# The last 64 rows of w_down as 128 half rows on all partitions, and no closing barrier

## The chip, the cores and the metric

The kernel runs on one core of a Trainium2 chip. The metric is the device time of one execution in microseconds (us). "Span" is the time from the first to the last recorded instruction of the core; the device time is longer than the span (1288.06 against 1286.26 us in the profiled run of the kernel before), and this text calls that difference the gap. A partition is one row of the on-chip memory: the first index of a tile in the code, 0 to 127. In the profile's lines PE is TensorE (PEld its weight loads), DVE is VectorE, ACT is ScalarE, POOL is GpSimd and SP is SyncE; a q behind the name means the engine's sequencer, which also issues the loads (SPq DMA_DIRECT2D in the profile, 328 to 548 ns each for the four loads of the feed-forward weights).

## The reference, cut to what matters

```python
xn = layernorm(x)                                    # x: [1, 1, 640]
att = softmax(q @ k.T / sqrt(128)) @ v               # 32 heads, 32768 cached keys and values of 128, bf16
y  = x + att.reshape(1, 1, 4096) @ wo \
       + (silu(xn @ w_gate) * (xn @ w_up)) @ w_down  # w_gate, w_up: [640, 1728]; w_down: [1728, 640]
```

One token is decoded. 554 MB of keys, values and weights are read once. 1728 hidden units are 13 full blocks of 128 and a rest of 64 (FM = 13, FB = 14, FL = 64 in the code).

## The kernel before

One DMA queue, issued by SyncE, streams everything in a fixed order into a ring of three slots. The end of the order is: last values, w_gate, w_up, w_down, then wo in six pieces. The loads of the feed-forward weights:

```python
e.dma_start(wg, B_w_gate.rearrange("(p c) n -> p (c n)", c=NCD)).then_inc(s_ffn[0], 16)
e.dma_start(wu, B_w_up.rearrange("(p c) n -> p (c n)", c=NCD)).then_inc(s_ffn[1], 16)
e.dma_start(flat[:, d0:d0 + FM * D], B_w_down[0:FM * 128, :].rearrange(
    "(p j) n -> p (j n)", j=FM)).then_inc(s_ffn[2], 16)
e.dma_start(wd[0:FL, FM, :], B_w_down[FM * 128:F, :]).then_inc(s_ffn[2], 16)   # 64 rows of 1280 B
# ... then six pieces of wo, of 8, 8, 8, 5, 2 and 1 rows of 640 per partition
e.wait_ge(s_fin, 2)
e.dma_start(out[0, 0:1, :].rearrange("o (c m) -> (o c) m", c=NCD), orow[:, :]).then_inc(s_out, 16)
```

TensorE multiplies with the weights as the stationary operand, so that all results are columns; the last block has only 64 rows:

```python
def down():
    t.wait_ge(s_ffn[2], 32)
    t.wait_ge(s_fd, 8)
    # ...
    for j in range(FB):
        n = 128 if j < FM else FL
        for c in range(NCD):
            t.matmul(acc[:, c:c + 1], lhsT=wd_v[0:n, j, c, :], rhs=hcol[0:n, j:j + 1], ...)
```

GpSimd builds constants at the start and at the end waits for the output write (`g.wait_ge(s_out, 16)`). After the engines' own streams the language puts a closing barrier: each engine drains and raises a semaphore, GpSimd collects the four and releases all. (In the records four engines have a drain, of 152 to 322 ns, and a semaphore record from 1273.2 to 1285.3 us; GpSimd's two follow at 1286.1 and 1286.2, the second one of the four at 1286.2.)

## Time and profile before

| what | value |
|---|---|
| time, median of 3 runs | 1288.11 us (1288.03 to 1288.64) |
| span, profiled run | 1286.3 us |
| bytes read | 554 MB at 431 GB/s over the span |
| last piece of wo in the queue | issued at 1254.4, landed 28.9 us later, about 1283.3 |
| output write issued | 1284.63 |
| GpSimd's branch to the closing barrier | 1285.9 |
| last record | 1286.26 |

Lines of the profile's page: the span; the mean busy share of the 16 DMA engines in 40 equal slices, in tenths; bytes.

```profile
span 1286.3 us, 9864 instructions
...
DMA  9999999999999999999999999999999999999998
...
HBM read 553.99 MB, written 0.00 MB: 431 GB/s over the span
```

The DMA row stays at 9, so there is no compute to be saved. Time can be won only where the queue moves fewer bytes than it could, or after its last byte.

The chain of waits at the end of the kernel before (start us, duration us, what):

```profile
1253.07 29.08 DMA ring<-in_A_wo_dram
1282.15 0.05 issue
1282.19 1.49 PE ps L414 x40
...
1283.81 0.17 DVE outb L603
...
1284.02 0.28 PE ps L439
...
1284.33 0.28 DVE orow L605
```

The chain is one long wait for wo. TensorE's last 40 matmuls stretch over 1.49 us because they contain the waits for the last two pieces: they start 27 ns apart, but 0.13 us where those land, at 1282.94 and 1283.33. Then comes a fixed tail.

Busy time by stretches of 1 us, kernel before. Columns: stretch; length; busy us and number of instructions of PE, PEld, DVE, ACT, POOL; granted clock; mean busy share of the DMA engines; GB/s moved.

```profile
1266.00:1267.00 1.00, 0.62 (x10) 0.63 (x11) 0.00 (x0) 0.00 (x0) 0.00 (x0) 0.50 1.05 449
...
1268.00:1269.00 1.00, 1.00 (x18) 0.97 (x18) 0.00 (x0) 0.20 (x1) 0.00 (x0) 0.50 1.01 329
1269.00:1270.00 1.00, 1.00 (x20) 1.00 (x20) 0.00 (x0) 0.00 (x0) 0.00 (x0) 0.50 1.01 323
1270.00:1271.00 1.00, 1.00 (x20) 1.00 (x19) 0.00 (x0) 0.00 (x0) 0.00 (x0) 0.50 0.96 340
1271.00:1272.00 1.00, 1.00 (x20) 1.00 (x20) 0.00 (x0) 0.00 (x0) 0.00 (x0) 0.50 0.98 399
```

The last two columns are the finding: for 3 us the DMA engines are fully busy and move a fifth less. That is when the 64-row piece, 80 KB, passes.

The records of the closing barrier, all on the line of the enclosing block (engine's sequencer, operation, count; ns min/median/max; start of the first and the last in us):

```profile
L79 SPq EVENT_SEMAPHORE  x2: 17/17/17, 1285.3 to 1286.2; - x2
L79 POOLq EVENT_SEMAPHORE  x2: 17/17/17, 1286.1 to 1286.2; - x2
...
L79 POOLq COMPARE_BRANCH  x1: 33/33/33, 1285.9 to 1285.9; - x1
```

SyncE is done at 1285.3 and is released at 1286.2. GpSimd (POOL) comes last, at 1285.9, since it waited for the output write, whose last semaphore update is at 1285.82.

### The profile page before, as it was taken

The numbers are of one execution on the slowest core, as the hardware profiler recorded it, in microseconds if no ns is written. First come the engines' busy times: TensorE is split into PE (matmuls) and PEld (weight loads), VectorE is DVE, ScalarE is ACT, GpSimd is POOL, SyncE is SP. The second block draws the span as 40 slices with busy tenths as digits, with TensorE's granted clock in tenths as the row PEclk, the third lists the DMA queues.
The fourth block names the chain that finished last, engine by engine and source line by source line (L and its number), as shares of the span: only waits on it lengthen the run. The fifth ranks groups of instructions, "written<-read, shape, count | busy, mean of one in ns | idle before, by whom it ended". The sixth has DMA issues, their size and how long they took to land.

```text
span 1286.3 us, 9864 instructions
## 1 busy us (share of the span) xinstructions
PE 1041.6 (81%) x5153; PEld 261.4 (20%) x3234; DVE 670.4 (52%) x409; ACT 52.2 (4%) x140; POOL 2.5 (0%) x17
## 2 busy tenths in 40 slices
PE   4599777789777788777798777788777798778797
PEld 1011112221112221112221112221112221112227
DVE  0855665445665445664446664446664446654440
ACT  2000000000000000000000000000000000000000
POOL 0000000000000000000000000000000000000000
PEclk9799888898888999888898888898888998888895
DMA  9999999999999999999999999999999999999998
GB/s 424 424 450 427 429 438 431 430 430 444 428 432 442 428 432 434 436 428 432 442 430 432 436 432 430 430 444 428 432 442 428 432 432 438 428 432 442 430 417 355
DMA packets 11192, 554.17 MB, mean 431 GB/s; under 512 B 1259, under 2 KB 1452, under 8 KB 1708
## 3 DMA queue, kind: packets, MB, share of 16 engines
q1 hardware_dynamic: 11178, 554.00, 99.7%
q8 instruction: 9, 0.15, 0.0%
q14 instruction: 3, 0.02, 0.0%
q10 hardware_dynamic: 2, 0.00, 0.0%
HBM read 553.99 MB, written 0.00 MB: 431 GB/s over the span
## 4 chain that ended last, share of the span: by engine, by line
DMA 53%; PE 30%; DVE 11%; issue 6%; DVEq 0%; SPq 0%
DMA ring<-in_A_k_cache_dram 51%; PE ps L327 17%; PE ps L295 11%; DVE ring L543 10%; DMA ring<-in_A_wo_dram 2%; PE ps L314 1%; PE ps L369 0%; PE ps L363 0%; PE ps L357 0%; PE ps L414 0%; SPq L239 0%; DVEq L543 0%; DVE sc L549 0%; DVE pmax L555 0%; DVEq L188 0%
## 5 line engine op out<-in xcount | busy, mean ns | idle before, releaser
L543 DVE TENSOR_TENSOR ring<-ring,qb 128x8192 bf16<-128x8192 bf16 x128 | 557.8, 4420 | 316.4 <-DMA ring<-in_A_k_cache_dram 316.4
L295 PE MATMUL ps<-ring,ident 128*128 128x512 bf16 x1920 | 496.4, 417 | 0.0
L327 PE MATMUL ps<-ring,P 128*4 128x512 bf16 x1984 | 443.3, 379 | 0.0
L314 PE MATMUL ps<-ring,ident 128*128 128x512 bf16 x128 | 55.9, 437 | 220.7 <-DVE ring L543 220.2
L327 PEld LDWEIGHTS ps<-ring,P 128*4 128x4 bf16 x1984 | 163.4, 85 | 237.8
L314 PEld LDWEIGHTS ps<-ring,ident 128*128 128x128 bf16 x128 | 12.6, 98 | 618.0 <-DVE ring L543 345.0
L549 DVE TENSOR_REDUCE sc<-ps 128x64 f32<-128x512 f32 x128 | 82.3, 684 | 62.6 <-PE ps L295 62.6
L561 DVE TENSOR_SCALAR negb<-ps 128x1 f32<-128x1 f32 x32 | 5.1, 158 | 108.4 <-PE ps L369 108.4
L466 ACT ACTIVATE P<-sc,negb 128x256 bf16<-128x256 f32 x32 | 16.2, 507 | 956.7 <-DVE negb L561 956.7
L558 DVE TENSOR_REDUCE m<-ps 1x1 f32<-1x128 f32 x32 | 8.9, 278 | 85.2 <-PE ps L363 85.2
L349 PEld LDWEIGHTS ps<-identf,o 4*128 4x128 f32 x248 | 30.6, 190 | 13.1 <-issue 13.1
L349 PE MATMUL ps<-identf,o 4*128 4x1 f32 x248 | 33.2, 251 | 0.0
L357 PEld LDWEIGHTS ps<-rsum,ones 128*128 128x128 f32 x64 | 12.1, 190 | 99.0 <-issue 98.2
L457 ACT ACTIVATE o<-ps,rzb 4x512 f32<-4x512 f32 x31 | 21.0, 678 | 6.2 <-PE ps L327 6.2
L287 PE MATMUL ps<-ring 128*128 128x512 bf16 x39 | 11.3, 458 | 10.9 <-DMA ring<-in_A_wq_dram 10.9
L462 ACT ACTIVATE ocol<-ps 128x1 f32 (+1 forms) x31 | 5.4, 173 | 222.2 <-PE ps L349 222.2
L555 DVE TENSOR_REDUCE pmax<-sc 128x1 f32<-128x256 f32 x32 | 13.4, 420 | 0.0
L363 PE MATMUL ps<-identf,pmax 128*1 128x128 f32 x64 | 12.2, 273 | 1.2 <-DVE pmax L555 1.2
L369 PE MATMUL ps<-m,ones 1*128 1x1 f32 x64 | 12.1, 256 | 0.4 <-DVE m L558 0.4
L369 PEld LDWEIGHTS ps<-m,ones 1*128 1x128 f32 x64 | 9.4, 182 | 14.2 <-issue 13.5
L393 PE MATMUL ps<-xn,ring 128*128 128x1 bf16 (+1 forms) x140 | 8.9, 198 | 1.6 <-issue 1.6
L531 DVE RECIPROCAL rzb<-ps 128x1 f32<-128x1 f32 x32 | 5.1, 159 | 8.1 <-PE ps L357 8.1
(62 smaller groups left out, 80.8 us busy)
## 6 DMA issues: line engine op xcount, KB each, us to landing
ring<-in_A_wq_dram SPq DMA_DIRECT2D x1, 5120.0 KB, 15.3
ring<-in_A_v_cache_dram SPq DMA_DIRECT2D x1, 4096.0 KB, 31.8
ring<-in_A_wo_dram SPq DMA_DIRECT2D x3, 1280.0 KB, 25.0
ring<-in_B_w_gate_dram SPq DMA_DIRECT2D x1, 2160.0 KB, 22.9
ring<-in_B_w_up_dram SPq DMA_DIRECT2D x1, 2160.0 KB, 27.7
ring<-in_B_w_down_dram SPq DMA_DIRECT2D x1, 2080.0 KB, 31.7
ring<-in_A_v_cache_dram SPq DMA_DIRECT2D x1, 2048.0 KB, 36.4
ring<-in_A_v_cache_dram SPq DMA_DIRECT2D x2, 1024.0 KB, 39.4
```

The source lines that it names most:

```text
L295: return t.add_instruction(mybir.InstMatmult(start_tensor_calc=False, stop_tensor_calc=stop, tile_size=(128, 128), tile_position=(0, 0), l ...
L314: t.matmul(ob, lhsT=ident[:, :], rhs=src, start=True, stop=False)
L327: mm = t.matmul(O, lhsT=P[:, h % PR, j:j + W], rhs=ring[:, s, j * DH:(j + W) * DH], start=(j == 0), stop=(j + W == NJ))
L349: mm = t.matmul(fold_ps, lhsT=o4[:, m * DH:(m + 1) * DH], rhs=identf[0:W, m:m + 1], start=(m == 0), stop=(m == W - 1))
L357: t.matmul(misc[:, 129:130], lhsT=ones[:, :], rhs=rsum[:, h % SR:h % SR + 1], start=True, stop=True).then_inc(s_z, 1)
L363: t.matmul(misc[0:1, 0:128], lhsT=pmax[:, h % SR:h % SR + 1], rhs=identf[:, :], start=True, stop=True).then_inc(s_t, 1)
L369: t.matmul(misc[:, 128:129], lhsT=ones[0:1, :], rhs=m1[0:1, h % SR:h % SR + 1], start=True, stop=True).then_inc(s_b, 1)
L457: a.activation(out=o4[:, :], in_=O, func=ACTF.Copy, scale=rzb[0:W, h % SR:h % SR + 1]).then_inc(s_o4, 1)
L466: a.activation(out=P[:, h % PR, :], in_=sc[:, :], func=ACTF.Exp, bias=negb[:, h % SR:h % SR + 1], scale=c_scale, accum_out=rsum[:, h % SR: ...
L543: v.tensor_tensor(out=kh, in0=kh, in1=q[:, None, :].to_broadcast([128, HF, DH]), op=ALU.mult).then_inc(s_mul, 1)
L549: v.tensor_reduce(out=sc[:, i * HF:(i + 1) * HF], in_=bank[i].rearrange("p (j e) -> p j e", e=G), axis=AX.X, op=ALU.add).then_inc(s_red, 1)
L555: v.tensor_reduce(out=pmax[:, h % SR:h % SR + 1], in_=sc[:, :], axis=AX.X, op=ALU.max).then_inc(s_max, 1)
```

## The change

Intent: let the last 64 rows of w_down use all 128 partitions, as the other loads of the feed-forward weights do, and let each engine end with its own stream. Row f becomes two half rows on partitions 2f and 2f + 1. Each hidden unit of the last block must then stand on two partitions, too. So VectorE doubles the last 64 columns of w_gate and w_up, and the last hidden column is masked by the parity of the partition into two columns, one for each half of the outputs. Core of the diff, with cuts:

```diff
-                        e.dma_start(wd[0:FL, FM, :], B_w_down[FM * 128:F, :]).then_inc(s_ffn[2], 16)
+                        e.dma_start(wdr, B_w_down[FM * 128:F, :].rearrange(
+                            "f (t n) -> (f t) n", t=2)).then_inc(s_ffn[2], 16)
 ...
+                    for half in range(2):
+                        a, b = half * (D // 2), (half + 1) * (D // 2)
+                        for c in range(a // 128, (b + 127) // 128):
+                            m0, m1 = max(a, c * 128), min(b, c * 128 + 128)
+                            t.matmul(acc[m0 - c * 128:m1 - c * 128, c:c + 1], lhsT=wdr[:, m0 - a:m1 - a],
+                                     rhs=hcol[:, FM + half:FM + half + 1],
+                                     start=False, stop=False, skip_group_check=True)
 ...
+                def twice(i):
+                    v.wait_ge(s_ffn[i], 16)
+                    v.tensor_copy(out=wt[i].rearrange("p c (f t) -> p c f t", t=2),
+                                  in_=(wg_v, wu_v)[i][:, :, FM * 128:F][:, :, :, None].to_broadcast(
+                                      [128, NCD, FL, 2])).then_inc(s_twice, 1)
 ...
+                v.tensor_reduce(out=par[:, :], in_=ident[:, :].rearrange("p (f t) -> p t f", t=2),
+                                axis=AX.X, op=ALU.add).then_inc(s_fd, 1)
 ...
+                v.tensor_scalar(out=hcol[:, FM:FM + 2], in0=par[:, :], scalar1=sg[:, 0, FM:FB],
+                                scalar2=ffn[:, FB + FM:2 * FB], op0=ALU.mult, op1=ALU.mult).then_inc(s_fd, 1)
 ...
+    nc.main_func.blocks[-1].instructions = []
```

The gate arithmetic also becomes one piece of 14 columns instead of two pieces (13 columns, and 64 rows of one).

More of the change, by code (lines that the diff above doesn't have):

```diff
@@ L98, in bass_parallel_sum__gqa_block_cached__swiglu_ffn__decode_kernel @@
         ot = sbt("ot", [128, OC], BF16)
-        hcol = sbt("hcol", [128, FB], BF16)
+        hcol = sbt("hcol", [128, FB + 1], BF16)
+        par = sbt("par", [128, 2], F32)
         sg = sbt("sg", [128, 2, FB], F32)
@@ L131, in bass_parallel_sum__gqa_block_cached__swiglu_ffn__decode_kernel @@
         s_att, s_fin = sem("att"), sem("fin")
+        s_twice = sem("twice")
         s_xr, s_or = sem("xr"), sem("orow")
@@ L160, in bass_parallel_sum__gqa_block_cached__swiglu_ffn__decode_kernel @@
         d0 = f0 + 2 * NCD * F
-        wd = flat[:, d0:d0 + FB * D].rearrange("p (j d) -> p j d", j=FB)
-        assert 2 * NCD * F + FB * D <= CE
+        wd = flat[:, d0:d0 + FM * D].rearrange("p (j d) -> p j d", j=FM)
+        wdr = flat[:, d0 + FM * D:d0 + FM * D + D // 2]
+        assert 2 * NCD * F + FM * D + D // 2 <= CE and 2 * FL == 128 and D % 2 == 0
         wg_v = wg.rearrange("p (c n) -> p c n", c=NCD)
@@ L165, in bass_parallel_sum__gqa_block_cached__swiglu_ffn__decode_kernel, with hidden @@
         wd_v = wd.rearrange("p j (c m) -> p j c m", c=NCD)
-        def hidden(w, c, j):
+        u0 = d0 + FM * D + D // 2
+        wt = [flat[:, u0 + i * NCD * 128:u0 + (i + 1) * NCD * 128].rearrange("p (c m) -> p c m", c=NCD)
+              for i in range(2)]
+        assert u0 + 2 * NCD * 128 <= f0 + CE
+        def hidden(i, c, j):
+            w = (wg_v, wu_v)[i]
             if j < FM:
                 return w[:, c, 0:FM * 128].rearrange("p (m j) -> p m j", j=FM)[:, :, j]
-            return w[:, c, FM * 128:F]
+            return wt[i][:, c, :]
         wo = flat[:, WO_S * CE:WO_S * CE + OC * D]
@@ L388, in hidden_part @@
                     t.wait_ge(s_ffn[i], 16)
-                    w = (wg_v, wu_v)[i]
                     for j in range(FB):
-                        n = 128 if j < FM else FL
+                        if j == FM:
+                            t.wait_ge(s_twice, i + 1)
                         for c in range(NCD):
-                            mm = t.matmul(ffn[0:n, i * FB + j:i * FB + j + 1], lhsT=hidden(w, c, j),
+                            mm = t.matmul(ffn[:, i * FB + j:i * FB + j + 1], lhsT=hidden(i, c, j),
                                           rhs=xn[:, c:c + 1], start=(c == 0), stop=(c == NCD - 1))
@@ L398, in down @@
                     t.wait_ge(s_ffn[2], 32)
-                    t.wait_ge(s_fd, 8)
-                    first = True
-                    for j in range(FB):
-                        n = 128 if j < FM else FL
+                    t.wait_ge(s_fd, 6)
+                    for j in range(FM):
                         for c in range(NCD):
-                            t.matmul(acc[:, c:c + 1], lhsT=wd_v[0:n, j, c, :], rhs=hcol[0:n, j:j + 1],
-                                     start=first, stop=False, skip_group_check=True)
-                            first = False
+                            t.matmul(acc[:, c:c + 1], lhsT=wd_v[:, j, c, :], rhs=hcol[:, j:j + 1],
+                                     start=(j == 0 and c == 0), stop=False, skip_group_check=True)
+                    for half in range(2):
[5 more added lines that the diff above has]
+                                     start=False, stop=False, skip_group_check=True)
                 def project():
@@ L489, in act @@
                 a.wait_ge(s_f, 1)
-                a.activation(out=sg[:, 0, 0:FB - 1], in_=ffn[:, 0:FB - 1], func=ACTF.Exp,
-                             scale=-1.0).then_inc(s_fa, 1)
-                a.activation(out=sg[0:FL, 0, FB - 1:FB], in_=ffn[0:FL, FB - 1:FB], func=ACTF.Exp,
-                             scale=-1.0).then_inc(s_fa, 1)
+                a.activation(out=sg[:, 0, :], in_=ffn[:, 0:FB], func=ACTF.Exp, scale=-1.0).then_inc(s_fa, 1)
             @block.vector
@@ L573, in dve @@
                 rz(H - 1)
+                def twice(i):
[3 more added lines that the diff above has]
+                                      [128, NCD, FL, 2])).then_inc(s_twice, 1)
+                twice(0)
                 h = H - 1
@@ L582, in dve @@
                                 in1=blk[:, None, :].to_broadcast([128, H, RB]), op=ALU.mult).then_inc(s_ob, 1)
-                v.wait_ge(s_fa, 2)
-                pieces = [(slice(0, 128), slice(0, FM)), (slice(0, FL), slice(FM, FB))]
-                n = 0
-                for stage in range(4):
-                    for p, f in pieces:
-                        fu = slice(FB + f.start, FB + f.stop)
-                        if stage == 0:
-                            ins = v.tensor_scalar(out=sg[p, 0, f], in0=sg[p, 0, f], scalar1=1.0, scalar2=None,
-                                                  op0=ALU.add)
-                        elif stage == 1:
-                            ins = v.reciprocal(out=sg[p, 1, f], in_=sg[p, 0, f])
-                        elif stage == 2:
-                            ins = v.tensor_tensor(out=sg[p, 0, f], in0=sg[p, 1, f], in1=ffn[p, f], op=ALU.mult)
-                        else:
-                            ins = v.tensor_tensor(out=hcol[p, f], in0=sg[p, 0, f], in1=ffn[p, fu], op=ALU.mult)
-                        ins.then_inc(s_fd, 1)
-                        n += 1
-                    v.wait_ge(s_fd, n)
+                twice(1)
+                v.tensor_reduce(out=par[:, :], in_=ident[:, :].rearrange("p (f t) -> p t f", t=2),
+                                axis=AX.X, op=ALU.add).then_inc(s_fd, 1)
+                v.wait_ge(s_fa, 1)
+                v.tensor_scalar(out=sg[:, 0, :], in0=sg[:, 0, :], scalar1=1.0, scalar2=None,
+                                op0=ALU.add).then_inc(s_fd, 1)
+                v.wait_ge(s_fd, 2)
+                v.reciprocal(out=sg[:, 1, :], in_=sg[:, 0, :]).then_inc(s_fd, 1)
+                v.wait_ge(s_fd, 3)
+                v.tensor_tensor(out=sg[:, 0, :], in0=sg[:, 1, :], in1=ffn[:, 0:FB], op=ALU.mult).then_inc(s_fd, 1)
+                v.wait_ge(s_fd, 4)
+                v.tensor_tensor(out=hcol[:, 0:FM], in0=sg[:, 0, 0:FM], in1=ffn[:, FB:FB + FM],
+                                op=ALU.mult).then_inc(s_fd, 1)
+                v.tensor_scalar(out=hcol[:, FM:FM + 2], in0=par[:, :], scalar1=sg[:, 0, FM:FB],
+                                scalar2=ffn[:, FB + FM:2 * FB], op0=ALU.mult, op1=ALU.mult).then_inc(s_fd, 1)
                 v.wait_ge(s_xr, 1)
```

## The prediction

> **What bounds it.** The kernel streams 554 MB at a mean of 431 GB/s over a 1286.3 us span, the page's DMA row at 9 tenths in nearly every slice: the DMA queue bounds it from start to end. The engines matter only after the last byte. In the chain of waits the end is: the projection weights (wo) land piece by piece (1282.15, then two smaller ones by about 1283.3), 40 last matmuls (1282.19 to 1283.68), one DVE add, one transposing matmul, one DVE cast, output DMA issued at 1284.63, GpSimd sees it landed at 1285.85, then the closing barrier: branch 1285.91, last semaphore records of all engines at 1286.2.
>
> **What the change removes.**
> 1. The 64-row piece of w_down (64 x 1280 B, partitions 0 to 63). It is only 80 KB, about 0.2 us at 430 GB/s, but the table by 1 us stretches shows 329, 323 and 340 GB/s in 1268 to 1271, with all engines busy, against 399 to 450 around it: about 250 KB missing, 0.6 us. Packet durations in the trace agree: in 1267 to 1272 packets take 0.73 us per DMA engine more than the shortest of their size, mostly the big neighbours (10240 B: 385 ns, up to 879 here), on all 16 engines. [...] As 128 half rows of 640 B [...] this goes away. Price: 128 small packets instead of 64; from 1280 B = 55 ns and 2560 B = 102 ns I estimate 32 ns for 640 B, so 0.25 instead of 0.22 us per engine. Net about -0.6 us, and it lies on the critical path: all of wo queues behind it.
> 2. The closing barrier: 1285.91 to 1286.26, about -0.3 us at the end of the span. What the runtime does outside the span (1288.06 less 1286.3 = 1.8 us) I expect about unchanged.
>
> **What it adds, off the critical path.** Two DVE copies of 128x640 bf16 (the like copy at the start took 0.82 us): one at about 1260 when w_gate has landed, before DVE is needed at 1262.5; one at about 1265.2 when w_up has landed, before PE needs it near 1268 to 1272. One 128x128 reduce in DVE's idle time. One more matmul in the down projection (71 for 70), two more waits on PE that are already met. The gate arithmetic loses four small DVE operations and one ACT operation. PE had 1.6 us of idle time (1278.6 to 1280.2) before it waited for wo; about 1 us of that remains.
>
> **Prediction.** 1288.1 - 0.6 - 0.35 - a little = 1287.0 us, range 1286.3 to 1287.7. Chance of faster by over 2%: 0.005; within 2%: 0.99; slower: 0.005.
>
> **What would show it.** Throughput in 1268 to 1271 at about 400 GB/s or more; wo landing 0.6 us earlier; PE still waiting for wo; the last record GpSimd's; span about 1285.3.
>
> **What would make it wrong.** The slow stretch may not come from the 64-row piece, or only engines with slack recover, so wo lands only 0.2 us earlier; an instruction fetch stall of PE (1.7 us idle at 1264.8) may move behind the down projection and eat the slack; the runtime's own end may wait as long as the barrier did, so its removal shows in the span but not in the time.

1288.1 less 0.6 (from the rates in 1268 to 1271), less 0.35 (the barrier), less a little comes to 1287.0 us. What the prediction calls an instruction fetch stall is an idle time of TensorE, from 1264.79 to 1266.38, that ended 1.4 us after an instruction packet of 16 KB (1263.90 to 1264.97); the profile names no releaser for it, so the link is the author's reading.

## The result, and the profile after

The changed kernel took 1287.47 us (median of 4 runs, 1287.11 to 1288.13), the kernel before 1288.07 us (1287.97 to 1288.64) in the same rounds: 0.6 us less, ratio 0.9995, interval 0.9978 to 1.0012. The span of the profiled run is 1285.6 us.

The same stretches in the kernel after:

```profile
1266.00:1267.00 1.00, 1.00 (x21) 1.00 (x19) 0.41 (x2) 0.00 (x0) 0.00 (x0) 0.50 1.09 466
...
1268.00:1269.00 1.00, 1.00 (x21) 1.00 (x19) 0.00 (x0) 0.00 (x0) 0.00 (x0) 0.50 1.02 416
1269.00:1270.00 1.00, 1.00 (x20) 1.00 (x19) 0.00 (x0) 0.00 (x0) 0.00 (x0) 0.50 0.98 391
1270.00:1271.00 1.00, 1.00 (x20) 1.00 (x19) 0.00 (x0) 0.00 (x0) 0.00 (x0) 0.50 1.05 431
```

The slow stretch is gone. The records of the single packets say the same: the loads' packets that start from 1267 to 1272 took 0.70 us per DMA engine (the sum over 16 engines, by 16) more than the shortest of their size before, and 0.06 us after. Linked end to start, the packets form 16 sequences; leaving out one packet beside an instruction fetch, each lost 0.62 to 0.77 us before, and at most 0.04 us after. What was added stays off the chain; VectorE's two copies, in the timeline after (start, duration, instruction, idle time before it and what ended that):

```profile
1260.26 0.82 DVE L588 COPY ring<-ring 128x640 bf16<-128x640 bf16 x1 [7.09 <-DMA ring<-in_B_w_gate_dram]
1265.40 0.82 DVE L588 COPY ring<-ring 128x640 bf16<-128x640 bf16 x1 [2.80 <-DMA ring<-in_B_w_up_dram]
```

They run in VectorE's idle time, each for the 0.82 us foreseen. The chain of waits after:

```profile
1253.03 28.77 DMA ring<-in_A_wo_dram
1281.80 0.05 issue
1281.85 1.49 PE ps L428 x40
```

It is the old chain with the wait for wo 0.35 us shorter (1282.15 to 1281.80). The prediction had 0.6. Part of the difference arises ahead of the changed piece. These are lines of the DMA view before (operation, KB, us from issue to landing; the issues' start times agree within 0.1 us):

```profile
ring<-in_B_w_gate_dram SPq DMA_DIRECT2D x1, 2160.0 KB, 22.9
...
ring<-in_A_wo_dram SPq DMA_DIRECT2D x1, 800.0 KB, 29.1
```

The same lines after:

```profile
ring<-in_B_w_gate_dram SPq DMA_DIRECT2D x1, 2160.0 KB, 23.2
...
ring<-in_A_wo_dram SPq DMA_DIRECT2D x1, 800.0 KB, 28.8
```

w_gate, which stands before the changed piece in the queue, landed 0.3 us later in this run. So the piece gave back about 0.6 us between w_gate's landing and wo's in this pair of profiles, and 0.3 of it had been lost before.

At the end the barrier's records are gone; this is all that is left on that line:

```profile
L79 POOLq COMPARE_BRANCH  x1: 33/33/33, 1285.5 to 1285.5; - x1
```

The span ends with GpSimd's branch: 0.7 us earlier in all, 0.38 of it the data and 0.32 the barrier (GpSimd's branch ended at 1285.944 before, the last record at 1286.259). But the time fell by only 0.6 us or less: the gap rose from 1.80 us (1288.06 less 1286.26) to 2.04 us (1287.60 less 1285.56). The experiments ask about both halves.

### The profile page after: what moved, and what is told of

Its sections match the earlier page's. It is cut to its first block, busy times and chain, and to the rows that moved or that the text cites. A ratio compares the mean times of both kernels' runs of the same rounds, so it can differ in the third digit from the quotient of the medians.

```text
span 1285.6 us, 9851 instructions
## 1 busy us (share of the span) xinstructions
PE 1042.0 (81%) x5154; PEld 260.9 (20%) x3235; DVE 672.2 (52%) x409; ACT 52.1 (4%) x139; POOL 2.5 (0%) x17
## 4 chain that ended last, share of the span: by engine, by line
DMA 53%; PE 28%; DVE 12%; issue 6%; SPq 0%; DVEq 0%
DMA ring<-in_A_k_cache_dram 51%; PE ps L337 17%; DVE ring L554 12%; PE ps L305 9%; DMA ring<-in_A_wo_dram 2%; PE ps L324 1%; PE ps L379 0%; PE ps L373 0%; PE ps L367 0%; PE ps L428 0%; SPq L249 0%; DVEq L554 0%; DVE sc L560 0%; DVE pmax L566 0%; DVE m L569 0%
## 5 line engine op out<-in xcount | busy, mean ns | idle before, releaser
L403 PE MATMUL ps<-xn,ring 128*128 128x1 bf16 x140 | 8.3, 196 | 1.3 <-issue 1.3
```

## The experiments

My theory of the load: the partitions that the 64 rows are written to, 0 to 63, slow them and their neighbours, not the size of the packets or the number of rows. Why they should was not shown: the reason that the recorded texts gave is cut from e4_rows_32_95 and x0_rows_0_63, and in the latter also a lower estimate for the ten copies that rested on it. In the trace of the kernel before, the piece's 64 packets form 16 runs of four, in which they start 47 to 84 ns apart, and each load of w_down raises its semaphore 16 times; I read that as four rows for each of the 16 DMA engines. Rivals: packet size or row count, the switch between transfers, or that all of the gain is the barrier. My theory of the end: the barrier's 0.32 us shows in the time; rival: the gap takes it back.

### Each half of the change alone, and both again

Edits, each against one of the two kernels:

```diff
 e1_no_barrier (the kernel before)
+    nc.main_func.blocks[-1].instructions = []
 e2_half_rows (the changed kernel)
-    nc.main_func.blocks[-1].instructions = []
 e3_both_again: the changed kernel, no edit
```

> Only the closing barrier is taken out; w_down's last 64 rows stay on partitions 0 to 63. My theory (the two parts add up, and the barrier's share shows in the measured time): span about 0.33 us shorter than before's 1286.3, time about 0.3 us shorter than the runs of before, 1267 to 1271 as slow as before (323 to 340 GB/s). Rival A (the runtime's own end waits as long): span 0.33 us shorter, time unchanged within 0.1 us. Rival B (the barrier is all of the gain): time 0.6 us shorter.

> Only the half rows, with the closing barrier kept. My theory: no slow stretch at 1267 to 1271; the last byte of wo lands 0.3 to 0.6 us earlier than in before, according to which DMA engines the instruction fetches of the tail hit; time 0.3 to 0.6 us shorter. Rival B (the barrier is all of the gain): time within 0.1 us of before.

> The changed kernel once more, as a control in the same rounds. My theory: time 0.6 to 0.9 us under before; if the shortfall against the predicted 1.05 us is only which DMA engine the instruction fetches hit, this profile's landing of w_gate (23.2 us after issue in the first profile of this kernel, 22.9 in before) may differ again, and the last wo landing moves with it. Sum rule: its gain equals that of e1_no_barrier plus that of e2_half_rows within 0.3 us.

### Whole rows on partitions 32 to 95

The load keeps its 64 packets of 1280 B. The compute takes 96 rows; 32 of the weight rows are zero. (A form with two matmuls of 32 rows each was not run.) Cut:

```diff
-                        e.dma_start(wd[0:FL, FM, :], B_w_down[FM * 128:F, :]).then_inc(s_ffn[2], 16)
+                        e.dma_start(wd[32:32 + FL, FM, :], B_w_down[FM * 128:F, :]).then_inc(s_ffn[2], 16)
-            return w[:, c, FM * 128:F]
+            return w[:, c, FM * 128 - 32:F]
 ...                                    # 64 becomes 96 rows in matmuls, exponential and gate arithmetic
+                v.memset(wd[0:32, FM, :], 0.0).then_inc(s_fd, 1)
+    nc.main_func.blocks[-1].instructions = []
```

> Whole rows again, 64 packets of 1280 B, but on partitions 32 to 95, computed with 96-row operands whose first 32 weight rows are zero, and no closing barrier. If the slow stretch comes from [...] (my theory), it is gone here too: packets of 10240 B at 385 to 395 ns, 400 GB/s or more at 1267 to 1271, and time as e3_both_again within 0.2 us or a little below. If it comes from the piece having 64 rows, or from its packet size, the stretch stays slow and the time is that of e1_no_barrier.

Measured in these rounds, five runs of each, before 1288.13 us (9 runs, 1287.92 to 1288.66):

| kernel | load of the 64 rows | barrier | time, median (range) | mean time less mean span |
|---|---|---|---|---|
| before | partitions 0 to 63 | yes | 1288.13 (1287.92 to 1288.66) | 1.81 |
| e1_no_barrier | partitions 0 to 63 | no | 1287.88 (1287.77 to 1288.29) | 1.98 |
| e2_half_rows | 128 half rows | yes | 1287.38 (1287.33 to 1287.42) | 1.80 |
| e3_both_again | 128 half rows | no | 1287.37 (1287.23 to 1287.47) | 2.00 |
| e4_rows_32_95 | partitions 32 to 95 | no | 1287.49 (1287.33 to 1287.72) | 2.03 |

With the barrier the half rows are worth 0.75 us, above the 0.3 to 0.6 expected for this run, and without it 0.51 us (e1_no_barrier against e3_both_again); the prediction had 0.6. That the barrier is all of the gain is refuted. Taking the barrier out as well adds 0.01 us, on the old load it adds 0.25: both little, neither the 0.35 predicted. The two gains add up within the 0.3 us expected (0.25 and 0.75 against 0.76 together). A good part of such differences is scatter in when the data lands: over the ten profiles of e1 to e8, before and after, the last piece of wo landed at 1283.33 (before) and 1283.21 (e1_no_barrier) with the old load, and at 1282.59 to 1282.98, mean 1282.77, in the eight with a new one. So the load is worth about 0.5 us, and 0.4 us lie between the ends of those eight. e1_no_barrier's stretches are as slow as before's (316, 312 and 321 GB/s from 1268 to 1271). In e3_both_again w_gate landed 22.9 us after its issue and the 800 KB piece of wo 28.6 us: the landing ahead of the piece did vary between two profiles of one kernel, as expected, and wo's moved with it.

e4_rows_32_95, stretches:

```profile
1268.00:1269.00 1.00, 1.00 (x20) 1.00 (x19) 0.00 (x0) 0.20 (x1) 0.00 (x0) 0.50 1.01 421
1269.00:1270.00 1.00, 1.00 (x20) 1.00 (x19) 0.00 (x0) 0.00 (x0) 0.00 (x0) 0.50 1.02 409
1270.00:1271.00 1.00, 1.00 (x20) 1.00 (x20) 0.00 (x0) 0.00 (x0) 0.00 (x0) 0.50 1.00 410
```

The rows, the packets and their number are those of the kernel before; of the load only the partitions changed, and the slow stretch is gone. (The barrier is out too, but in e1_no_barrier, without it, the stretch stays slow.) Row count and packet size are ruled out as the cause. This also does the change's work without the doubled columns, the mask and the half rows.

### The load by itself, ten times over

Ten more copies of the piece behind w_down into dead space, in the kernel before, the down projection waiting for all; the first piece stays on partitions 0 to 63 in all four. x0 and x1 differ in the destination alone, x2 also in the size of the packets, x3 in the bytes:

```diff
+                        for i in range(10):
+                            x = d0 + FB * D + i * D        # D // 2 for x2
+                            e.dma_start(DEST, SOURCE).then_inc(s_ffn[2], 16)
-                    t.wait_ge(s_ffn[2], 32)
+                    t.wait_ge(s_ffn[2], 32 + 160)
 x0: DEST flat[0:FL, x:x + D]         SOURCE the 64 rows
 x1: DEST flat[32:32 + FL, x:x + D]   SOURCE the 64 rows
 x2: DEST flat[:, x:x + D // 2]       SOURCE the 64 rows as 128 half rows
 x3: DEST flat[:, x:x + D]            SOURCE the last 128 rows
```

> Before, with the 64-row piece loaded ten more times into dead space behind w_down, each copy on partitions 0 to 63, and the down projection waiting for all of them: the cost of the layout by itself. My theory [...]: [...] up to 0.8 us each (8 us) if every copy disturbs its neighbours as the single one did. Rival (the slow stretch belongs to the switch from one transfer to the next, not to the partitions): about the same as x1_rows_32_95.

> The same ten extra copies, the same 64 packets of 1280 B each, on partitions 32 to 95. My theory: only the packets' own time, 4 packets of 55 ns per engine and copy, 0.22 us, so 2.2 us for ten, with no packet slowed. Rival (the number of rows or the switch is the cause): as slow as x0_rows_0_63.

> The same ten extra copies as 128 half rows of 640 B on all partitions, the layout of the change. Estimate 8 packets of 29 to 32 ns per engine and copy: 0.25 us, 2.5 us for ten, a few tenths more than x1_rows_32_95.

> Ten extra copies of twice the bytes: 128 rows of 1280 B on all partitions (160 KB each). My theory: 8 packets of 55 ns per engine and copy, 0.44 us, 4.4 us for ten: about what x0_rows_0_63 takes for half of the bytes, or less. Rival (bytes and rows set the cost): twice x0_rows_0_63.

The packets in these estimates are those of the first two traces: in the kernel before 16 runs of four packets of 1280 B, 55 ns each where nothing slows them; in the changed kernel 16 runs of eight packets of 640 B, 32 ns each and starting 28 to 29 ns apart.

Measured against before, 1288.06 us in these rounds; the last column is the median time less that, by ten. The packet durations are read from the trace's DMA records from the 1240th us on, all packets of that size.

| run | time, median (range) | packets, median ns | us per extra copy |
|---|---|---|---|
| x0_rows_0_63 | 1294.96 (1294.54 to 1295.21) | 1280 B: 107 | 0.69 |
| x1_rows_32_95 | 1290.91 (1290.07 to 1291.83) | 1280 B: 56 | 0.29 |
| x2_half_rows | 1291.34 (1291.25 to 1291.55) | 640 B: 32 | 0.33 |
| x3_rows_0_127 | 1293.63 (1293.54 to 1293.86) | 1280 B: 59 | 0.56 |

Stretches of 2 us in x0_rows_0_63:

```profile
1268.00:1270.00 2.00, 2.00 (x37) 2.00 (x36) 0.00 (x0) 0.20 (x1) 0.00 (x0) 0.50 0.99 190
1270.00:1272.00 2.00, 2.00 (x35) 1.99 (x35) 0.00 (x0) 0.00 (x0) 0.00 (x0) 0.50 1.10 191
1272.00:1274.00 2.00, 0.25 (x5) 0.17 (x4) 0.93 (x8) 0.23 (x2) 0.00 (x0) 0.50 1.10 181
1274.00:1276.00 2.00, 0.00 (x0) 0.00 (x0) 0.00 (x0) 0.00 (x0) 0.00 (x0) 0.50 1.08 203
```

The same stretches in x1_rows_32_95:

```profile
1268.00:1270.00 2.00, 2.00 (x34) 1.97 (x34) 0.00 (x0) 0.20 (x1) 0.00 (x0) 0.50 0.97 300
1270.00:1272.00 2.00, 2.00 (x36) 2.00 (x36) 0.00 (x0) 0.00 (x0) 0.00 (x0) 0.50 1.12 373
1272.00:1274.00 2.00, 0.97 (x16) 0.87 (x14) 0.65 (x6) 0.23 (x2) 0.00 (x0) 0.50 1.06 435
```

On partitions 0 to 63 the rate falls to 181 to 203 GB/s and stays there, with busy engines; the same packets on 32 to 95 take half as long each. Twice the bytes on 128 partitions (x3) take 0.56 us, less than the 0.69 us of the 64 rows. So it is the destination, not the switch between transfers, the packets or the bytes. By the time per copy x1 loads its 81920 B at 287 GB/s and x0 at 119. (The four runs of x1 scatter from 0.20 to 0.38 us per copy; even the slowest is well below the fastest of x0, 0.65.) What the runs show is that the partitions decide, not why. Partitions 64 to 127 were not run. Half rows cost 0.04 us more than whole rows on 32 to 95, near the estimate of 0.03 us. All four lie above their packets' own time (x1 to x3 by 0.06 to 0.09 us; x0, at 4 packets of 107 ns, by 0.26 us), which nothing here explains.

### Who waits for the output write

The gap of 1.8 us with the barrier and 2.0 us without says that the time after the last record depends on how the engines end. So the wait for the output write was moved, from GpSimd to SyncE, to ScalarE, or to all engines, in the changed kernel:

```diff
-                g.wait_ge(s_out, 16)          # GpSimd; kept in e7
+                e.wait_ge(s_out, 16)          # e5, e7, e8: SyncE, after it issued the write
+                a.wait_ge(s_out, 16)          # e6, e7: ScalarE
+                t.wait_ge(s_out, 16)          # e7: TensorE; and the same on VectorE
-    nc.main_func.blocks[-1].instructions = [] # e8 alone: the barrier is back
```

> The changed kernel, but SyncE instead of GpSimd waits for the output write at the end. So far the time less the span was 1.81 us with the closing barrier (14 runs) and 2.00 us without (19 runs), so 0.19 of the barrier's 0.33 us came back outside the span. If the runtime's own end simply needs its engines together, whoever is last, the gap stays at 2.00 and the time at 1287.4. If it depends on which engine arrives last (rival), the gap differs by 0.1 us or more, and the time with it.

> The same with ScalarE as the only engine that waits for the output write. If whoever is last does not matter: gap 2.00, time 1287.4 within 0.1 us of e5_sp_waits. Rival: a gap that differs from e5_sp_waits and from the changed kernel.

> The changed kernel, but all five engines wait for the output write and end together, without the barrier's two steps. If the 0.19 us came back because the other engines were no longer together at the end of the program, the gap falls to 1.8 us again at a span as short as without the barrier, and the time is about 0.2 us under the changed kernel's, 1287.2. If the gap is set by something else, it stays at 2.00.

> The half rows with SyncE waiting for the output write, as in e5_sp_waits, but with the closing barrier kept: the fourth corner of barrier yes/no by who waits. The times so far fit a rule that the program ends about 1.9 to 2.0 us after GpSimd's last record, and only 1.4 to 1.6 us after another engine's last record where GpSimd is done long before. In the barrier GpSimd collects and releases, so it is among the last again: expected gap 1.8 to 1.9 us and time 0.7 to 0.8 us under before, as e2_half_rows. Rival (it is the wait in GpSimd itself that is slow, not its coming last): gap and time fall as in e5_sp_waits, plus the barrier's 0.33 us: about 1.0 us under before.

Five runs each. e2 and e3, e5 to e7, and e8 are three sets of rounds on three chips, so each is put against before of its own rounds (1288.13, 1288.06 and 1288.05 us). All have the half rows.

| kernel | barrier | waits for the output | time, median (range) | less before | mean gap | time less the end of GpSimd's last record |
|---|---|---|---|---|---|---|
| e2_half_rows | yes | GpSimd | 1287.38 (1287.33 to 1287.42) | -0.75 | 1.80 | 1.89 |
| e3_both_again | no | GpSimd | 1287.37 (1287.23 to 1287.47) | -0.76 | 2.00 | 2.03 |
| e5_sp_waits | no | SyncE | 1286.74 (1286.57 to 1286.84) | -1.32 | 1.42 | GpSimd done at 4.3 us |
| e6_act_waits | no | ScalarE | 1286.76 (1286.69 to 1287.08) | -1.30 | 1.61 | GpSimd done at 4.4 us |
| e7_all_wait | no | all five | 1287.26 (1287.16 to 1287.35) | -0.80 | 1.87 | 1.93 |
| e8_sp_waits_barrier | yes | SyncE | 1287.49 (1287.32 to 1287.60) | -0.56 | 1.84 | 1.89 |

The last column is taken from the profiled run of each. The end of the program in e5_sp_waits:

```profile
L79 POOLq COMPARE_BRANCH  x1: 33/33/33, 4.3 to 4.3; - x1
L79 SPq COMPARE_BRANCH  x1: 33/33/33, 1285.4 to 1285.4; - x1
```

And in e8_sp_waits_barrier, where GpSimd collects for the barrier:

```profile
L79 POOLq EVENT_SEMAPHORE  x2: 17/17/17, 1285.3 to 1285.4; - x2
L79 POOLq COMPARE_BRANCH  x1: 33/33/33, 4.4 to 4.4; - x1
```

GpSimd left its stream at 4.3 us in the one; in the other it came back into play for the barrier. Wherever GpSimd is among the last, the program ends 1.89 to 2.06 us after its last record (the first profile of the changed kernel, too: 1287.60 less 1285.56 is 2.04). Where it has been done for long, the program ends 1.4 us after SyncE or 1.6 us after ScalarE. My expectation that only the last engine's being together with the others matters was wrong: in e7_all_wait the gap did fall, to 1.87 us (before has 1.86 in these rounds), but it gains only 0.04 us over e3_both_again, each against its own before, while 0.2 was expected, and e5_sp_waits, for which 2.00 us had been expected if the order did not matter, gains over 0.5 us. e8_sp_waits_barrier has the gap that the rule said, 1.84 us; its gain of 0.56 us is below the 0.7 to 0.8 expected. With the barrier kept, moving the wait is worth nothing.

The scatter of the data can be left out by timing each profiled run from the issue of the output write to the end of the program. With the barrier this is 3.42 to 3.46 us in seven profiles (before, e2, e8 and the four with ten copies), without it 3.25 to 3.37 us in four (after, e1, e3, e4), and 3.24 us in e7, 2.89 us in e6 and 2.65 us in e5. So taking out the barrier is worth about 0.1 us, and moving the wait as well about 0.45 us more with ScalarE and 0.7 us with SyncE. The times of e5 and e6 hardly differ all the same: in e6's profile the output write was issued 0.3 us earlier.

So e5_sp_waits is faster than both kernels: 1.32 us under before, where the changed kernel is 0.6 to 0.76 us under it. What happens between the last record and the end is not in the trace, so why it takes longer with GpSimd is open. TensorE or VectorE as the last engine, and rows on 32 to 95 together with SyncE's wait, were not run.

## Why the prediction was right or wrong

The time fell in the stated range (1287.47 in 1286.3 to 1287.7), but the predicted gain was about 1.1 us and the measured one 0.6 us (0.76 in the control). The range is wider than the gain itself: a gain of 0.4 us would have lain in it, so hitting it says little. By step:

1. The DMA queue bounds the kernel and the engines matter only after the last byte: right. The chain has the same form, and TensorE waits for wo in both.
2. The slow stretch comes from the 64-row piece, by the partitions that it is written to, and goes away: right. Shown by e4_rows_32_95 (of the load only the partitions moved) and the ten-fold copies (0.69 us on 0 to 63 against 0.29 us on 32 to 95); why these partitions are slow was not shown. One detail was misread: the packet of 879 ns is not slowed by the piece. In all five of the profiles before, after, e2, e3 and e4 at least one such packet of 10240 B (879 or 880 ns) starts as an instruction fetch of 16 KB ends. The piece slowed 57 packets of 10240 B to between 425 and 602 ns, and 18 of 16640 B from 620 to between 714 and 855 ns; its own 64 took 55 to 88 ns.
3. Worth 0.6 us on the critical path: right in size on the whole, 0.75 us in e2_half_rows against before, 0.51 us without the barrier and about 0.5 us in the landings of all profiles, but only 0.35 us in the first profile of the changed kernel, where w_gate had already landed 0.3 us later. The landing that counts is the last of 16: the semaphore of the 800 KB piece of wo was raised 16 times from 1280.28 to 1282.15 before and from 1279.65 to 1281.80 after, and TensorE went on 0.04 to 0.05 us after the last. My reading, which no run tests: these are 16 DMA engines, and instruction fetches may hit one that is late already. In both profiles the DMA records show five fetches of 16 KB between 1250 and 1283, of 1.06 to 1.12 us each, and a packet of the data that starts as one of them ends takes about 0.5 us longer (1192 ns for 644, 1113 for 620, 879 for 385). That variation, some 0.3 us, belonged into the range of this term.
4. The barrier, "about -0.3 us at the end of the span": right for the span (0.32 us), and mis-sized for the time. The step that failed is "What the runtime does outside the span ... I expect about unchanged": the gap rose from 1.81 to 2.00 us, so that 0.19 of 0.32 us came back; measured in the time, taking out the barrier was worth 0.25 us on the old load and 0.01 us on the new, and about 0.1 us from the output write to the end, where 0.35 was predicted. The prediction named this among what could make it wrong.
5. The added work is off the critical path: right. The copies took 0.82 us each in VectorE's idle time, and the version without them, e4_rows_32_95, is not faster. (The gate arithmetic loses three VectorE operations, not four.)

## What to carry to other kernels

In a kernel bound by its DMA queue, look for stretches where the DMA engines are fully busy and the rate is low; here a small piece on partitions 0 to 63 cost several times what its bytes take (about 0.5 us where 80 KB take 0.2 at 430 GB/s), since it slowed its neighbours too (57 packets of 10240 B took 425 to 602 ns instead of 385), and moving its rows to partitions 32 to 95 cured that as well as a reshaped load (1287.49 against 1287.37 us), with less added code. What comes off the recorded span at the very end need not come off the time (here 0.19 of 0.32 us came back): compare the time less the span. In these runs it paid to let SyncE or ScalarE instead of GpSimd be the last one to wait and to drop the barrier in which GpSimd collects; only the two together were worth over 0.5 us.
